# A linear-attention block whose feature blocks are cut at three heads, with the engines' order written anew

## The chip, the cores and the metric

The kernel runs on one core of one Trainium2 chip. The metric is device time in microseconds (us): the kernel before took 280.55 us, the median of three runs (280.23, 280.55 and 280.56). The profile is that of one execution. The engines are called as in the profile: PE multiplies matrices (PEld are its weight loads), DVE, ACT and POOL are the vector, scalar and general engines, SP issues DMAs; a q behind an engine's name marks what its sequencer does, such as issuing a DMA.

## The reference, cut to what matters

```python
def _A_ref(x, wqkv, w_phi, wo):          # x: 1 x 2048 x 640, H = 32 heads of Dh = 20
    q, k, v = ...                        # x @ wqkv, by heads
    pq = jnp.einsum("bhsd,hdf->bhsf", q, w_phi)
    pk = jnp.einsum("bhsd,hdf->bhsf", k, w_phi)
    phi_q = jnp.concatenate([_softmax(pq, axis=-1), _softmax(-pq, axis=-1)], axis=-1)
    phi_k = jnp.concatenate([_softmax(pk, axis=-1), _softmax(-pk, axis=-1)], axis=-1)
    kv = jnp.einsum("bhsf,bhsd->bhfd", phi_k, v)
    z  = jnp.einsum("bhsf->bhf", phi_k)
    num = jnp.einsum("bhqf,bhfd->bhqd", phi_q, kv)
    den = jnp.einsum("bhqf,bhf->bhq", phi_q, z)[..., None] + 1e-6
    o = num / den
    return (lambda x, *d: x.transpose(*d))(o, 0, 2, 1, 3).reshape(B, S, D) @ wo
...
h = x + _A_ref(_layernorm(x, axis=-1), A_wqkv, A_w_phi, A_wo)
h2 = h + _B_ref(_layernorm(h, axis=-1), B_w_gate, B_w_up, B_w_down)   # ((x@wg) * (x@wu)) @ wd, F = 1536
```

A head has 20 scores and, by softmax of both signs, 40 features. All heads together have 1280 features per token, and 32 x 21 columns of V with a column of ones, which gives the denominator.

## The kernel before, in words

The 2048 tokens are 16 tiles (t = 0 to 15) of 128. Everything that is matrix work goes through one helper, `mms` (line 570 is its matmul), so the profile names nearly all matmuls L570, and they are told apart by their tiles and columns. The weight of a matmul is always 128x128; what differs is the number of columns that move.

The work falls into units, and a unit's name is what the lists of the order use:

- `in`: first loads. On SP's list, in the order in which the code makes them: rows 0 of W_k (`load_wnat(1, (0, 1))`, 160 KB), rows 1 and 2 (320 KB), the transposed x tiles xT0 and xT1 (DMA transposes, `load_xT`), W_v (`load_wv`, 800 KB), xT2, xT3. On ACT's list: rows 3 and 4 of W_k (320 KB), then W_phi's rows (`Wrows`), then a first exp. On DVE and POOL: constants, masks and the block-diagonal `Phi`, which is made from `Wrows`. `lT4` to `lT15` are the further xT tiles, `lx0` to `lx3` the x rows by four tiles, `lwq`, `lwo`, `lg`, `lu`, `ld` weights, `t0` to `t4` DMA transposes of W_q.
- `wk`, ten entries on PE: for each of five row blocks of W_k a sum of its columns and a turn (transposes on PE, L659). Blocks 0 and 1 are copied out by DVE (L697) and ACT (L700, ACT's first `wk`). `lwq` writes W_q into the buffer `Wnat` that W_k lies in, and so comes after all five turns.
- `x0` to `x4`: W_k times `Phi`, evicted to `Wp`. `wv`, `c0` to `c4`: W_v is centred. `s0, s2, s4, s8, s12`: layer-norm sums of the batches of tiles from xT (`s0` is tiles 0 and 1, `s2` tiles 2 and 3). `y0` to `y4`: W_q times `Phi`.
- `k`t: scores of K (ten matmuls of 320 columns), a maximum (DVE), two exps (ACT) into `phik`; `K`t normalizes them (DVE sum and reciprocal, POOL product). `v`t: V, into `vaug`. `A`t: K^T V of two tiles, accumulated over all tiles in one PSUM buffer. `Aout`: its eviction with the mask `Gk` and the epsilon, to `KVsb` (L905, L908).
- `q`t and `Q`t: the same for the queries, into `eq`, which two DMA transposes bring to `phiqT`. `n`t: phi_q KV, division, and the turn to `oT`. `h`t: the product with W_o, the residual and sums for the second layer norm. `f`b.ft.j: gate and up product of four (or two) tiles, `d`t and `e`t: down product, residual, store.

The features of a tile are cut at every 128, without regard to heads, so a block touches up to four heads (SL = 4): its K^T V has 4 x 21 = 84 columns. `HQ[c]` is the first head of block c, and `Gk` zeroes what belongs to other heads. Ten blocks make a tile, in K^T V (`kv_mm`) as in phi_q KV (`num`).

The order is written out by hand for each engine in `ORDER`: an entry takes the next operation of that unit on that engine. `Prog.place` goes through the lists with a cost model (durations t, latencies) to choose buffers, and `Prog.finish` puts semaphore waits where an operation depends on one of another engine. Each engine works through its list in order, so an entry that waits holds what stands behind it. A DMA issue that waits holds the later issues of its engine too. A load's landing is, in the cost model,

```python
land = o.at or max(s + 2.3, fabric) + o.bytes
```

with `at` a landing time given in the code for the first loads (`load_wnat(1, (3, 5), "ACT", at=4.3)` and the others of `in`). DMAs go through rings of eight semaphores: an issue waits for the eighth one before it of its ring.

Of the kernel before, what the change touches and what calls it, by code (L numbers as in the profile page):

```python
# [34 lines left out]

# [342 lines left out]
def _build(ctx, nc, A_x, A_wqkv, A_w_phi, A_wo, B_w_gate, B_w_up, B_w_down, out):  # L378
# [437 lines left out]
    def softexp(v, t, i, dst, regs_, use=()):
        mx = lambda: PS[v.i][:, 1, MXC:MXC + 1]
        g.op("DVE", lambda e: e.tensor_reduce(out=mx(), in_=PS[v.i][:, :, 0:HALF], axis=AX.XY, op=ALU.max,  # L818
                                              apply_absolute_value=True, negate=True), rd=v.R, wr=[R_mx[i]], use=[v],
             t=0.735, lat=0.85)  # L820
        g.op("DVE", lambda e: e.tensor_tensor(out=nb[:, i:i + 1], in0=mx(), in1=rs[:, t:t + 1], op=ALU.mult),  # L821
             rd=[R_mx[i], R_rs[t]], wr=[R_nb[i]], use=[v], t=0.1, lat=0.24)
        for s in range(2):
            sc = rs if s == 0 else nrs
            g.op("ACT", lambda e, s=s, sc=sc: e.activation(  # L825
                out=signed(dst(), s), in_=PS[v.i][:, :, 0:HALF].rearrange("p b (h f) -> p b h f", f=DH), func=ACT.Exp,
                bias=nb[:, i:i + 1], scale=sc[:, t:t + 1]), rd=v.R + [R_nb[i], R_rs[t], R_nrs[t]], wr=[regs_[s]], use=[v] + list(use),
                t=0.775, lat=0.92)
# [68 lines left out]
    def kv_out():  # L897
        U("Aout")
        v = KVBUF
        for k in range(2):  # L900
            dst = KVsb[:, NC * KVW * k:NC * KVW * (k + 1)].rearrange("p (c h e) -> p c h e", c=NC, e=E21)

            def psv(k=k):
                return PS[v.i][:, k, 0:NC * KVW].rearrange("p (c h e) -> p c h e", c=NC, e=E21)
# [211 lines left out]
```

## Time and profile before

| | |
|---|---|
| runs | 280.23, 280.55, 280.56 us |
| span of the profiled execution | 278.3 us |
| PE busy | 274.1 us, 2239 matmuls |
| DVE / ACT / POOL busy | 165.3 / 134.5 / 106.2 us |
| warm-up matmuls at the start of PE | 0.83 to 5.04 us |
| first scores of K (128x320) | from 12.64 us |
| K^T V (128x84, 160 matmuls) | in groups from 64 to 74.4 us |
| phi_q KV (128x84, 160 matmuls) | 74.4 to 191.1 us |

A line of the timeline gives start and length in us, the engine, the line, the operation, what it writes and reads, and how many instructions are merged; a bracket tells how long the engine was idle before and what ended that. A line of groups ends in total busy time, mean length of one in ns, and idle time before. A line of DMA issues ends in the size of one and the median time from issue to landing. A matmul's length includes its passage through the array, so that the spacing of starts, not the length, is what a stream of them costs.

### The profile page before, as it was taken

To read this page: it belongs to the slowest core of one execution; us is meant where nothing else is said; L and a number is where in the kernel's file an instruction comes from. 1 tells how busy PE (TensorE), PEld (TensorE's weight loads), DVE (VectorE), ACT (ScalarE), POOL (GpSimd) and SP (SyncE) were. 2 spreads that over 40 slices of the span, in tenths; PEclk is the share of its full clock that TensorE was granted. 3 is DMA by queue.
4 is the path that set the end of the run, shared out by engine and by line. 5 is a ranking of instruction groups with operands and counts; after the bars stand their busy time and mean duration, and the time that the engine had idled before them with its cause. 6 is when DMAs were issued, how large, how long until landed. Compare 5 with 4: busy or idle time off the path is not lost.

```text
span 278.3 us, 5485 instructions
## 1 busy us (share of the span) xinstructions
PE 274.1 (99%) x2239; PEld 186.9 (67%) x2239; DVE 165.3 (59%) x314; ACT 134.5 (48%) x229; POOL 106.2 (38%) x150
## 2 busy tenths in 40 slices
PE   8999999999999999999999999999999999999995
PEld 8877777777878888877656555776464444447773
DVE  1999999999999876588545845313251222324011
ACT  3478999899666465421764413113244314340132
POOL 5438889899732240061320903142100000250252
PEclk9999999999999999999999999999999999999999
DMA  7988886008864617969643031544312000000112
GB/s 196 277 148 185 126 271 251 0 2 236 167 82 110 97 27 155 336 100 198 88 111 82 24 71 27 123 89 97 94 30 20 0 0 2 0 24 24 49 47 71
DMA packets 65193, 28.06 MB, mean 101 GB/s; under 512 B 55697, under 2 KB 63889, under 8 KB 65169
## 3 DMA queue, kind: packets, MB, share of 16 engines
q1 hardware_dynamic: 64240, 27.37, 43.8%
q10 hardware_dynamic: 928, 0.35, 0.5%
q8 instruction: 17, 0.28, 0.4%
q14 instruction: 8, 0.06, 0.1%
HBM read 11.82 MB, written 2.62 MB: 52 GB/s over the span
## 4 chain that ended last, share of the span: by engine, by line
PE 95%; DMA 2%; SPq 1%; DVE 1%; issue 0%
PE ps L570 95%; DMA Wp<-in_A_wqkv_dram 2%; SPq L471 1%; PE ps L482 0%; DVE outb L1022 0%; SPq L467 0%; DVE KVsb L905 0%; DVE KVsb L908 0%; DVE nb L821 0%
## 5 line engine op out<-in xcount | busy, mean ns | idle before, releaser
L570 PE MATMUL ps<-phik,Wgu 128*128 128x512 bf16 (+1 forms) x600 | 107.5, 336 | 0.0
L570 PEld LDWEIGHTS ps<-phik,Wgu 128*128 128x128 bf16 x600 | 58.2, 98 | 43.6 <-DVE phik L981 1.8
L570 PE MATMUL ps<-Wp,xT 128*128 128x320 bf16 x480 | 69.0, 299 | 0.0
L981 DVE TENSOR_TENSOR phik<-ps,gate 128x512 bf16<-128x512 f32 (+1 forms) x60 | 33.9, 577 | 55.3 <-PE ps L570 50.1
L570 PE MATMUL ps<-vaug,phik 128*128 128x320 bf16 (+3 forms) x544 | 60.0, 270 | 0.0
L979 ACT ACTIVATE gate<-ps 128x512 bf16<-128x512 f32 (+1 forms) x60 | 29.8, 510 | 59.7 <-PE ps L570 40.8
L570 PEld LDWEIGHTS ps<-Wp,xT 128*128 128x128 bf16 x480 | 45.9, 98 | 17.6 <-DVE phik L981 0.2
L570 PEld LDWEIGHTS ps<-vaug,phik 128*128 128x128 bf16 x544 | 43.7, 97 | 15.7
L839 POOL TENSOR_TENSOR phik<-phik,Rk 128x1280 bf16<-128x1280 bf16 x16 | 37.5, 2356 | 5.1 <-DVE Rk L838 4.8
L997 POOL TENSOR_TENSOR outb<-t,x_all 128x640 bf16<-128x640 f32 x12 | 16.8, 1397 | 56.9 <-ACT t L994 49.6
L994 ACT ACTIVATE t<-ps,mh,rs 128x640 f32<-128x640 f32 x12 | 10.6, 882 | 37.1 <-PE ps L570 37.1
L818 DVE TENSOR_REDUCE ps<-ps 128x1 f32<-128x640 f32 x32 | 26.3, 824 | 1.6 <-PE ps L570 1.2
L858 DVE TENSOR_REDUCE Sq<-eq 128x64 f32<-128x1280 bf16 x16 | 23.5, 1471 | 3.5 <-ACT eq L825 3.5
L825 ACT ACTIVATE eq<-ps,nb,rs 128x640 bf16<-128x640 f32 x16 | 14.2, 885 | 20.3 <-DVE nb L821 11.7
L836 DVE TENSOR_REDUCE Ssum<-phik 128x64 f32<-128x1280 bf16 x16 | 23.5, 1474 | 0.0
L964 POOL TENSOR_SCALAR vpe<-shc 128x1 f32<-128x1 f32 x16 | 3.0, 190 | 52.7 <-ACT junk L563 51.7
L869 POOL TENSOR_TENSOR eq<-eq,rq 128x640 bf16<-128x640 bf16 x16 | 20.2, 1270 | 0.5
L864 POOL TENSOR_TENSOR rq<-Sq,rq 128x32 f32<-128x32 f32 x16 | 4.0, 254 | 41.5 <-DVE rq L863 41.5
L563 ACT ACTIVATE junk<-x_all 128x640 bf16<-128x640 bf16 x20 | 14.6, 732 | 4.4 <-DVE x_all L958 4.4
L825 ACT ACTIVATE phik<-ps,nb,rs 128x640 bf16<-128x640 f32 x16 | 14.2, 889 | 2.4 <-DVE nb L821 2.4
L825 ACT ACTIVATE phik<-ps,nb,nrs 128x640 bf16<-128x640 f32 x16 | 14.3, 894 | 0.0
L825 ACT ACTIVATE eq<-ps,nb,nrs 128x640 bf16<-128x640 f32 x16 | 14.2, 885 | 0.0
(86 smaller groups left out, 235.8 us busy)
## 6 DMA issues: line engine op xcount, KB each, us to landing
x_all<-in_A_x_dram SPq DMA_DIRECT2D x4, 640.0 KB, 5.2
out_dram<-outb SPq DMA_DIRECT2D x15, 160.0 KB, 1.8
Wgu<-in_B_w_gate_dram SPq DMA_DIRECT2D x1, 1920.0 KB, 11.1
Wgu<-in_B_w_up_dram SPq DMA_DIRECT2D x1, 1920.0 KB, 9.1
vaug<-in_B_w_down_dram SPq DMA_DIRECT2D x1, 1920.0 KB, 8.3
Wp<-in_A_wqkv_dram SPq DMA_DIRECT2D x1, 800.0 KB, 4.9
phiqT<-in_A_wqkv_dram SPq DMA_DIRECT2D x1, 800.0 KB, 6.5
Wo<-in_A_wo_dram SPq DMA_DIRECT2D x1, 800.0 KB, 6.8
```

The lines of the kernel that those rows point to most:

```text
L563: g.op("ACT", lambda e: e.activation(out=junk[:, v.i, :], in_=in_, func=func, accum_out=acc), rd=rd, wr=wr, use=[v], t=0.73, lat=0.97)
L570: ins = e.matmul(o_, lhsT=l_, rhs=r_, start=s_, stop=p_, skip_group_check=True)
L818: g.op("DVE", lambda e: e.tensor_reduce(out=mx(), in_=PS[v.i][:, :, 0:HALF], axis=AX.XY, op=ALU.max, apply_absolute_value=True, negate=Tru ...
L825: g.op("ACT", lambda e, s=s, sc=sc: e.activation(out=signed(dst(), s), in_=PS[v.i][:, :, 0:HALF].rearrange("p b (h f) -> p b h f", f=DH), ...
L836: g.op("DVE", lambda e: e.tensor_reduce(out=Ssum[:, vs.i, :], in_=x, axis=AX.X, op=ALU.add), rd=R_phik[t], wr=vs.R, use=[vs], t=1.39, lat=1.5)
L839: g.op("POOL", lambda e: e.tensor_tensor(out=x, in0=x, in1=Rk[:, vr.i, :].unsqueeze(2).to_broadcast([P, 2 * H, DH]), op=ALU.mult), rd=vr.R ...
L858: g.op("DVE", lambda e: e.tensor_reduce(out=Sq[:, vs.i, :], in_=eq[:, b.i, :].rearrange("p (g f) -> p g f", f=DH), axis=AX.X, op=ALU.add), ...
L869: return e.tensor_tensor(out=x, in0=x, in1=rq[:, vr.i, :].unsqueeze(2).to_broadcast([P, H, DH]), op=ALU.mult)
L979: g.op("ACT", lambda e: e.activation(out=gate[:, vg.i, 0:P * n], in_=PS[v.i][:, 0, 0:P * n], func=ACT.Copy), rd=[v.R[0]], wr=vg.R, use=[v, ...
L981: g.op("DVE", lambda e: e.tensor_tensor(out=hhT[:, hb, ft, sl], in0=PS[v.i][:, 1, 0:P * n], in1=gate[:, vg.i, 0:P * n], op=ALU.mult), rd=[ ...
L994: g.op("ACT", lambda e: e.activation(out=t32[:, v3.i, :].rearrange("p (b n) -> p b n", b=2), in_=PS[v.i][:, :, 0:HALF], func=ACT.Identity, ...
L997: g.op("POOL", lambda e: e.tensor_tensor(out=outb[:, vo.i, :], in0=t32[:, v3.i, :], in1=x_all[:, t, :], op=ALU.add), rd=v3.R + [R_h[t]], w ...
```

## The change

Each block of 128 features now holds three heads and a pad of 8 features ahead of them: eleven blocks a tile (the last with two new heads; in K^T V it takes head 29 once more), 3 x 21 = 63 columns each. For K the pad is the 8 features ahead of the block in `BK`, for which 8 zero columns are put ahead of tile 0; for Q, `eq` is laid out with the pad, filled once with ones, and `Gk` has zero rows for it. In `num` the last block has two heads, 42 columns. The scores of the queries are split into 300 and 340 columns across two PSUM banks, their exps into two pieces for each sign, the transposes into five and six blocks. `KVsb` now lies where `Phi` was, and there is one `junk` buffer in place of two. The lists of the order are new for all five engines.

```diff
 DF = 2 * DH
-NQ = 2 * NC
-HQ = [P * c // DF for c in range(NQ)]
-SL = 4
-KVW = SL * E21
+HW = 3
+NQ = 11
+PADW = P - HW * DF
+KVW = HW * E21
+WB = ((0, 5), (5, NQ))
+HB = 5 * HW
...
     "PE":
-        "warm wk wk wk wk wk wk wk wk wk wk s0 s0 x1 x1 x3 wv wv x2 x0 x0 s2 s2 x4 k0 k0 k0 k0 k0 k1 k3 wm k2 v0 v2 s4 s4 "
+        "warm wk wk wk wk wk wk wk wk wk wk s0 x1 s0 x1 x3 wv wv x2 x0 x0 s2 x4 s2 k0 k0 k0 k0 k0 k1 k3 wm s4 s4 s4 s4 k2 k7 v2 "
...
-        "k12 v9 v12 v15 v14 k14 k15 A0 A2 A4 v8 q2 q3 A6 v10 A0 A2 A8 q5 A10 A4 A12 A6 A8 A10 A14 A12 A14 n1 n0 n0 n1 q7 "
+        "v15 k13 k15 v8 q2 v13 v10 q3 A0 A2 A4 A0 q5 A2 A6 A4 A8 A10 A6 A8 A12 A10 A14 A12 A14 n1 n0 n1 q7 n0 n1 q4 n0 h1 h0 n2 "
...
     "ACT":
-        "in in in wk wk wk x2 x0 x4 k0 k0 wm k1 k1 k3 k3 k2 k2 v0 wq3 v2 v3 wq1 v7 k7 k7 y2 k4 k4 v5 s12 v4 y0 s12 s12 k6 "
+        "wk in in wk wk in x2 x0 x4 s12 s12 k0 k0 wo2 wm k1 k1 k3 k3 k2 k2 wq1 v2 wq3 k7 k7 v3 v7 v0 k4 k4 y0 v5 y2 k6 s12 k6 "
...
     "SP":
-        "in in in in in in in lwq t4 lT7 lT4 t2 lT5 lT6 t3 t1 t0 lx3 lT10 lT15 lT9 lT11 lT8 lT13 lT14 lT12 lx0 lwo lg Q0 "
...
+        "lT7 in lT5 lx3 lT4 in lwo lT6 lwq lT8 lT15 t4 t0 t1 t2 t3 lT10 in lT11 in lT9 lT12 in in lx2 in lT14 lT13 lu Q0 lx1 lg "
...
-    BK = sb([P, 2 * NT * D], BF16, "phik")
+    BK = sb([P, PADW + 2 * NT * D], BF16, "phik")
...
-    affine([R_Gk], Gk[:, :, :], [[P - 3 * DF, NC], [-DF, SL]], 0, 1)
-    affine([R_Gk], Gk[:, :, :], [[3 * DF - P, NC], [DF, SL]], DF - 1, -1)
+    affine([R_Gk], Gk[:, :, :], [[0, 6], [-DF, HW]], -PADW, 1)
+    affine([R_Gk], Gk[:, :, :], [[0, 6], [DF, HW]], PADW + DF - 1, -1)
+    pool_op(lambda e: e.memset(eq[:, :, :].rearrange("p b (w n) -> p b w n", n=P)[:, :, :, 0:PADW], 1.0), 0.4, wr=[R_pad])
+    pool_op(lambda e: e.memset(eq[:, :, (NQ - 1) * P + PADW:(NQ - 1) * P + PADW + DF], 1.0), 0.2, app=[R_pad])
+    pool_op(lambda e: e.memset(BK[:, 0:PADW], 0.0), 0.1, wr=[R_pad0])
...
+            for k, (to, of, n) in enumerate(pieces):
+                g.op("ACT", lambda e, s=s, sc=sc, to=to, of=of: e.activation(
+                    out=to(s), in_=of(), func=ACT.Exp, bias=nb[:, i:i + 1], scale=sc[:, t:t + 1]),
...
+        for k, (w0, w1) in enumerate(WB):
+            transpose(lambda w0=w0, w1=w1: phiqT[:, bb, w0:w1, P * tt:P * (tt + 1)], lambda w0=w0, w1=w1: eq[:, b.i, P * w0:P * w1],
+                      b.R + [R_pad], [R_phiqT[bb][k][tt]], [b], t=0.254 * (w1 - w0), size=0.214 * (w1 - w0))
...
-                for c in range(NC * k, NC * (k + 1)):
-                    lo = HQ[c]
-                    col = KVW * (c - NC * k)
+                for w in range(w0, w1):
+                    h0 = min(HW * w, H - HW)
                     for t in range(t0, t1):
-                        o_ = (t * H + lo) * E21
-                        lst.append((PS[v.i][:, k, col:col + KVW], phik[:, t, P * c:P * (c + 1)], BV[:, o_:o_ + KVW], first, False))
+                        k0, o_ = 2 * D * t + HW * DF * w, (t * H + h0) * E21
+                        if w == NQ - 1:
+                            k0 -= DF
+                        lst.append((PS[v.i][:, k, KVW * (w - w0):KVW * (w - w0 + 1)], BK[:, k0:k0 + P], BV[:, o_:o_ + KVW], first, False))
...
-                for c in range(NC * b0, NC * b1):
-                    bk = c // NC
-                    col = E21 * (HQ[c] - HH2 * bk)
-                    lst.append((PS[v.i][:, bk, col:col + KVW], phiqT[:, bb, c, P * tt:P * (tt + 1)], KVsb[:, KVW * c:KVW * (c + 1)],
-                                c % NC == 0, False))
+                for bk in range(b0, b1):
+                    for w in range(*WB[bk]):
+                        k0 = KVW * w + (E21 if w == NQ - 1 else 0)
+                        o_ = base + KVW * w
+                        n = KVW * (w + 1) - k0
+                        lst.append((flat(v)[:, o_:o_ + n], phiqT[:, bb, w, P * tt:P * (tt + 1)], KVsb[:, k0:k0 + n], w == WB[bk][0], False))
```

Between these, the other lists (DVE, POOL, and the rest of the three above) are replaced as a whole; which operations they hold, apart from the added ones, is the same. The landing times `at` of the first loads are not touched.

More of the change, by code (lines that the diff above doesn't have):

```diff
@@ L425, in _build @@
     Rk = sb([P, 2, 2 * H], FP32, "Rk")
-    Sq = sb([P, 2, 2 * H], FP32, "Sq")
-    rq = sb([P, 2, H], FP32, "rq")
+    Sq = sb([P, 2, 2 * HW * NQ], FP32, "Sq")
+    rq = sb([P, 2, HW * NQ], FP32, "rq")
     rden = sb([P, 2, H], FP32, "rden")
-    phik = BK[:, :].rearrange("p (t n) -> p t n", t=NT)
+    Phi = PK[:, :].rearrange("p (a n) -> p a n", a=NC)
+    KVsb = PK[:, 0:NQ * KVW]
+    phik = BK[:, PADW:PADW + 2 * NT * D].rearrange("p (t n) -> p t n", t=NT)
     pq = phiqT[:, :, :, :].rearrange("p b c n -> p (b c n)")
@@ L824, in softexp @@
             sc = rs if s == 0 else nrs
[L825 to L828, printed above, removed]
+            for k, (to, of, n) in enumerate(pieces):
+                g.op("ACT", lambda e, s=s, sc=sc, to=to, of=of: e.activation(
+                    out=to(s), in_=of(), func=ACT.Exp, bias=nb[:, i:i + 1], scale=sc[:, t:t + 1]),
+                    rd=v.R + [R_nb[i], R_rs[t], R_nrs[t]], use=[v] + list(use),
+                    t=0.095 + 0.00106 * n, lat=0.235 + 0.00107 * n, **{"app" if k else "wr": [regs_[s]]})
     def keys(t, after=()):
         U("k%d" % t)
-        softexp(proj(t, 1, after), t, t, lambda: phik[:, t, :], R_phik[t])
+        v = proj(t, 1, after)
+        softexp(v, t, t, lambda: PS[v.i][:, :, 0:HALF],
+                [(lambda s: signed(phik[:, t, :], s), lambda: PS[v.i][:, :, 0:HALF].rearrange("p b (h f) -> p b h f", f=DH), D)],
+                R_phik[t])
         U("K%d" % t)
@@ L851, in queries, with score, feat @@
         U("q%d" % t)
-        v = proj(t, 0, after)
+        v = Buf(p_ps, 2)
+        cut = HB * DH
+        g.op("PE", lambda e: mms(e, [(flat(v)[:, 512 - cut:512] if bk == 0 else flat(v)[:, 512:512 + D - cut], xT[:, t, c, 0:P],
+                                      Wp[:, c, cut * bk:cut + (D - cut) * bk], c == 0, c == NC - 1)
+                                     for c in range(NC) for bk in range(2)]),
+             rd=[R_xT[t]] + R_Wp[0], wr=v.R, use=[v], t=1.3575, lat=1.5075, after=after)
         bb, tt = (t // 4) % 2, t % 4
         b = Buf(p_eq, 2)
-        softexp(v, t, NT + t, lambda: eq[:, b.i, :], b.R, [b])
+        def score(lo, hi):
+            return flat(v)[:, 512 - cut + lo:512 - cut + hi]
+        def feat():
+            return eq[:, b.i, :].rearrange("p (w n) -> p w n", n=P)[:, :, PADW:P]
+        softexp(v, t, NT + t, lambda: score(0, D),
+                [(lambda s: feat()[:, 0:NQ - 1, :].rearrange("p w (h s f) -> p s w h f", s=2, f=DH)[:, s],
+                  lambda: score(0, 2 * cut).rearrange("p (w h f) -> p w h f", h=HW, f=DH), 2 * cut),
+                 (lambda s: feat()[:, NQ - 1, DF:].rearrange("p (h s f) -> p s h f", s=2, f=DH)[:, s],
+                  lambda: score(2 * cut, D).rearrange("p (h f) -> p h f", f=DH), D - 2 * cut)], b.R, [b])
         vs, vr = Buf(p_Sq), Buf(p_rq)
         U("Q%d" % t)
-        g.op("DVE", lambda e: e.tensor_reduce(out=Sq[:, vs.i, :], in_=eq[:, b.i, :].rearrange("p (g f) -> p g f", f=DH),
-                                              axis=AX.X, op=ALU.add), rd=b.R, wr=vs.R, use=[b, vs], t=1.4, lat=1.5)
+        g.op("DVE", lambda e: e.tensor_reduce(out=Sq[:, vs.i, :].rearrange("p (w g) -> p w g", w=NQ),
+                                              in_=feat().rearrange("p w (g f) -> p w g f", f=DH),
+                                              axis=AX.X, op=ALU.add), rd=b.R + [R_pad], wr=vs.R, use=[b, vs], t=1.44, lat=1.54)
         def sums(k):
@@ L867, in f @@
         def f(e):
-            x = eq[:, b.i, :].rearrange("p (h s f) -> p s h f", s=2, f=DH)[:, 1, :, :]
-            return e.tensor_tensor(out=x, in0=x, in1=rq[:, vr.i, :].unsqueeze(2).to_broadcast([P, H, DH]), op=ALU.mult)
-        g.op("POOL", f, rd=vr.R + [b.R[1]], wr=[b.R[1]], use=[b, vr], t=1.25)
-        for k in range(2):
-            transpose(lambda k=k: phiqT[:, bb, NC * k:NC * (k + 1), P * tt:P * (tt + 1)], lambda k=k: eq[:, b.i, D * k:D * (k + 1)],
-                      b.R, [R_phiqT[bb][k][tt]], [b])
+            x = feat().rearrange("p w (h s f) -> p s w h f", s=2, f=DH)[:, 1]
+            return e.tensor_tensor(out=x, in0=x, in1=rq[:, vr.i, :].rearrange("p (w h) -> p w h", h=HW).unsqueeze(3).to_broadcast(
+                [P, NQ, HW, DH]), op=ALU.mult)
+        g.op("POOL", f, rd=vr.R + [b.R[1], R_pad], wr=[b.R[1]], use=[b, vr], t=1.29)
+        for k, (w0, w1) in enumerate(WB):
+            transpose(lambda w0=w0, w1=w1: phiqT[:, bb, w0:w1, P * tt:P * (tt + 1)], lambda w0=w0, w1=w1: eq[:, b.i, P * w0:P * w1],
+                      b.R + [R_pad], [R_phiqT[bb][k][tt]], [b], t=0.254 * (w1 - w0), size=0.214 * (w1 - w0))
     KVBUF = Buf(p_ps, 2)
@@ L899, in kv_out, with psv @@
         v = KVBUF
[L900 to L904, printed above, removed]
-            g.op("DVE", lambda e, psv=psv, dst=dst: e.tensor_tensor(
-                out=dst[:, :, :, 0:DH], in0=psv()[:, :, :, 0:DH], in1=Gk[:, :, :].unsqueeze(3).to_broadcast([P, NC, SL, DH]), op=ALU.mult),
-                rd=[v.R[k], R_Gk], app=[R_KV[k]], use=[v], t=0.5, lat=0.6)
-            g.op("DVE", lambda e, psv=psv, dst=dst: e.scalar_tensor_tensor(
-                out=dst[:, :, :, DH], in0=psv()[:, :, :, DH], scalar=0.5 * EPS_DEN, in1=Gk[:, :, :], op0=ALU.add, op1=ALU.mult),
+        for k, (w0, w1) in enumerate(WB):
+            n = HW * (w1 - w0)
+            dst = KVsb[:, KVW * w0:KVW * w1].rearrange("p (h e) -> p h e", e=E21)
+            gk = Gk[:, :, :].rearrange("p w h -> p (w h)")[:, 0:n]
+            def psv(k=k, n=n):
+                return PS[v.i][:, k, 0:E21 * n].rearrange("p (h e) -> p h e", e=E21)
+            g.op("DVE", lambda e, psv=psv, dst=dst, gk=gk, n=n: e.tensor_tensor(
+                out=dst[:, :, 0:DH], in0=psv()[:, :, 0:DH], in1=gk.unsqueeze(2).to_broadcast([P, n, DH]), op=ALU.mult),
+                rd=[v.R[k], R_Gk], app=[R_KV[k]], use=[v], t=0.07 + 0.0213 * n, lat=0.18 + 0.0213 * n)
+            g.op("DVE", lambda e, psv=psv, dst=dst, gk=gk: e.scalar_tensor_tensor(
+                out=dst[:, :, DH], in0=psv()[:, :, DH], scalar=0.5 * EPS_DEN, in1=gk, op0=ALU.add, op1=ALU.mult),
                 rd=[v.R[k], R_Gk], app=[R_KV[k]], use=[v], t=0.09, lat=0.25)
@@ L928, in f @@
                 return mms(e, lst)
[L929 to L930 removed]
+            n = sum(WB[bk][1] - WB[bk][0] for bk in range(b0, b1)) * 0.0288 + 0.015
+            g.op("PE", f, rd=R_KV[b0:b1] + [R_phiqT[bb][k][tt] for k in range(b0, b1)], wr=v.R[b0:b1], use=[v], t=n, lat=0.15 + n)
         for b0, b1 in halves:
[L932 to L935 removed]
@@ L937, in rd_ @@
[L937 to L944 removed]
+            h0, h1 = (0, HB)[b0], (0, HB, H)[b1]
@@ L1067, in _build @@
         kv_mm(t, t + 2)
+    g.alias(R_KV, R_Phi)
     kv_out()
```

52 lines of the change are left out of this document (25 added, 27 removed), and 77 rows, old and new, of the table ORDER.

## The prediction, on record before the run

> **What bounds the kernel now.** I read the page first, then the chain of waits in order of time, then busy time by stretches, and last the timelines of the engines in the first microseconds.
>
> ```profile
> span 278.3 us, 5485 instructions
> PE 274.1 (99%) x2239; PEld 186.9 (67%) x2239; DVE 165.3 (59%) x314; ACT 134.5 (48%) x229; POOL 106.2 (38%) x150
> ```
>
> The span is 278.3 us and the runs have a median of 280.55, so 2.25 us lie around the span; I add my terms to 280.55, as if the profiled execution were the median one. PE is busy all the time, but matmuls overlap their tails, so that alone does not say that PE's columns are the limit. The chain of waits does:
>
> ```profile
> 0.79 0.40 SPq L467
> ...
> 4.38 4.94 DMA Wp<-in_A_wqkv_dram
> 9.32 0.05 issue
> 9.37 27.97 PE ps L570 x283
> ...
> 74.38 0.58 DVE KVsb L905
> ...
> 84.13 190.70 PE ps L570 x1322
> ...
> 274.85 1.02 DVE outb L1022 x2
> ```
>
> (columns: start, length, what.) Up to 9.32 us the end is set by SP's issues and by the landing of W_v; from 9.37 to 274.85 by PE's own stream, with one hole, where the two Aout evictions stand at 74.4. Busy time in the stretches before and after that hole:
>
> ```profile
> core 0: us, PE busy (x) PEld busy (x) DVE busy (x) ACT busy (x) POOL busy (x), PEclk, DMA share, GB/s
> 9.37:74.36 64.99, 64.95 (x689) 49.89 (x689) 63.61 (x118) 55.27 (x87) 53.26 (x56) 1.00 0.69 163
> 75.17:274.85 199.68, 199.60 (x1416) 128.25 (x1417) 96.69 (x178) 75.95 (x137) 48.40 (x74) 1.00 0.35 75
> ```
>
> PE has no slack in either (64.95 of 64.99, 199.60 of 199.68). Two things follow: every PE microsecond saved is a microsecond, and **whatever delays the start of PE's stream can't be caught up later**.
>
> **The matmuls that change.** Timeline of PE:
>
> ```profile
> 66.90 1.52 PE L570 MATMUL ps<-Wp,xT 128*128 128x320 bf16 x10
> 68.26 1.30 PE L570 MATMUL ps<-vaug,phik 128*128 128x84 bf16 x30
> 69.40 1.52 PE L570 MATMUL ps<-Wp,xT 128*128 128x320 bf16 x10
> ...
> 81.58 0.55 PE L570 MATMUL ps<-KVsb,phiqT 128*128 128x84 bf16 x10
> 81.97 1.52 PE L570 MATMUL ps<-Wp,xT 128*128 128x320 bf16 x10
> 40.41 0.64 PE L570 MATMUL ps<-ones,xT 128*128 128x1 bf16 x20
> ```
>
> ```profile
> L570 PE MATMUL ps<-ones,xT 128*128 128x1 bf16 x20 | 0.6, 163 | 0.0
> ```
>
> From start to the next group's start: 320 columns 1.36/10 = 136 ns; 84 columns 1.14/30 = 38 ns in K^T V and 0.39/10 = 39 ns in phi_q KV. The slope between is 98/236 = 0.415 ns a column, so 63 columns are 38 - 21 x 0.415 = 29.3 ns. From below, 20 matmuls of one column, each with its own weights, take (0.64 - 0.16)/19 = 25 ns each, the 0.16 being the length of the last one; from above, no gain a piece, 38 ns. K^T V per tile: 10 x 38 = 380 -> 11 x 29.3 = 322. phi_q KV: the eleventh has 42 columns, taken as 25: 390 -> 318. Over 16 tiles: 16 x (58 + 72) = **-2.1 us**. Ends: at 25 ns each -3.6, at 38 ns each +1.0.
>
> The Trainium skill, "TensorE: Matmul & The Clock Gate", section "LDWEIGHTS (loading the stationary operand)", speaks against this edit: a weight load takes its 128 columns divided by 1.2 GHz, 107 ns, however few columns follow. By it eleven loads instead of ten would cost 32 x 107 ns = +3.4 us (an estimate from that page). The trace doesn't bear it out as a spacing: twenty loads with one column each are spaced 25 ns.
>
> **The other parts of the edit.** Aout: four evictions of fewer heads, and in the new order the first half is complete three PE groups ahead of the end (A12, A14 of the other half between), so the hole of 0.8 us at 74.4 shrinks: -0.3 (between 0 and -0.8). Queries: two activations become four (600 and 40 of 640 elements), so 32 short ones more; the row below gives about 0.2 us each, 6.4 us of ACT. The six-block transpose instead of five adds a fifth of 1.27 us to 16 SP issues, 4 us of SP. DVE's sum over 66 groups instead of 64 and POOL's product over 33 heads instead of 32 add 3%, and three memsets on POOL lie where it waits for W_phi. After 75 us ACT is busy 75.95 of 199.68 and SP waits for data; PE's stream covers all this. Ahead of Aout four tiles' queries would add 8 x 0.2 = 1.6 us to ACT, which has 64.99 - 55.27 = 9.7 idle: 0, and +1.6 without that cover.
>
> ```profile
> L797 ACT ACTIVATE Wo<-wsum 128x1 bf16<-128x1 f32 x5 | 1.0, 220 | 0.0
> ```
>
> **The new order at the head, the large term.** Here each DMA issue counts. SP and ACT issue in the order written. Before:
>
> ```profile
> 0.79 0.87 SPq L467 DMA_DIRECT2D phiqT<-in_A_wqkv_dram  x2
> 1.72 2.62 SPq L471 DMA_TRANSPOSE xT<-in_A_x_dram  x2
> 4.38 0.59 SPq L467 DMA_DIRECT2D Wp<-in_A_wqkv_dram  x1
> 5.01 2.55 SPq L471 DMA_TRANSPOSE xT<-in_A_x_dram  x2
> 7.60 0.58 SPq L467 DMA_DIRECT2D phiqT<-in_A_wqkv_dram  x1
> 22.81 12.10 SPq L471 DMA_TRANSPOSE xT<-in_A_x_dram  x8
> 0.78 0.45 ACTq L467 DMA_DIRECT2D phiqT<-in_A_wqkv_dram  x1
> 6.18 0.70 ACT L700 ACTIVATE phiqT<-ps 128x640 bf16<-128x640 bf16 x1 [2.90 <-PE ps L659]
> ```
>
> So a transpose holds SP for 1.31 us at the head and 1.51 in a long row; a plain load for 0.45 to 0.63. Landing, in us from the issue:
>
> ```profile
> x_all<-in_A_x_dram SPq DMA_DIRECT2D x4, 640.0 KB, 5.2
> Wp<-in_A_wqkv_dram SPq DMA_DIRECT2D x1, 800.0 KB, 4.9
> phiqT<-in_A_wqkv_dram ACTq DMA_DIRECT2D x1, 320.0 KB, 3.7
> phiqT<-in_A_wqkv_dram SPq DMA_DIRECT2D x1, 320.0 KB, 4.3
> xT<-in_A_x_dram SPq DMA_TRANSPOSE x16, 4.4
> phiqT<-in_A_wqkv_dram SPq DMA_DIRECT2D x1, 160.0 KB, 2.9
> ```
>
> And PE's head:
>
> ```profile
> 0.83 4.21 PE L570 MATMUL ps<-const-bfloat16-1.0 128*128 128x128 bf16 x38 [0.83 <-PEq L1101]
> 5.55 0.29 PE L570 MATMUL ps<-ones,phiqT 128*128 128x1 bf16 x5
> 6.58 0.27 PE L570 MATMUL ps<-ones,phiqT 128*128 128x1 bf16 x5
> 7.11 0.44 PE L659 MATMUL ps<-ident,phiqT 128*128 128x128 bf16 x5
> 12.64 3.57 PE L570 MATMUL ps<-Wp,xT 128*128 128x320 bf16 x25
> ```
>
> In the new lists SP begins lT7, W_k rows 0, lT5, lx3, lT4, W_k rows 1-2, lwo, lT6, lwq, lT8, lT15, t4, t0, t1, t2, t3, lT10, xT0, lT11, xT1, lT9, lT12, W_v, xT2, lx2, xT3; and ACT does wk's copy of row block 1 *ahead* of its load of W_k rows 3-4. Followed through:
>
> 1. W_k rows 1-2 are issued after three transposes (3.9), a load of 0.45 and one of 0.6 at 0.79 + 5.1 = 5.9, and land 4.3 later: 10.2.
> 2. PE turns block 1, ACT copies it: 6.18 - 5.55 = 0.63 and 0.70, so ACT issues rows 3-4 at 11.5; landed at 15.2. Before, that issue stood at 0.78.
> 3. PE turns blocks 3 and 4: 7.11 + 0.44 - 6.58 = 0.97, to 16.2. lwq overwrites W_k's buffer and so waits for this; **everything behind it on SP waits too**, xT0 to xT3 and W_v among it, for which PE waits. lwq is out at 16.8.
> 4. Eight transposes (lT8 to lT10) at 1.31 to 1.51, say 1.45: xT0 is issued at 28.4.
> 5. Five more (xT0, lT11, xT1, lT9, lT12), 7.25: W_v at 35.7, landed 40.6.
> 6. W_v's 0.63, xT2 1.45, lx2 0.6: xT3 is issued at 38.4, landed 42.8 by the median, 43.9 if it queues behind lx2's 5.2 us. PE's order has s2 on xT2 and xT3 ahead of k0, and from W_v to k0 it has 12.64 - 9.37 = 3.3 us of work, 43.9. k0 starts at 43.7, against 12.64: **+31.1 us**, and nothing behind it has slack.
>
> Ends: with 1.31 a transpose, 2.9 for rows 1-2, k0 is at 39.9 (+27.3); with 1.55, 5.2 for every landing and a queue behind lx2, at 46.5 (+33.9).
>
> After a wait the matmuls may be slow again: the first 38 of 128 columns take 4.05/38 = 107 ns, about twice what 0.415 ns a column gives (53). A second such start costs at most the same 2.0 us; 0 if the 3.3 us of work ahead of k0 bring the speed back. I take +1.0. The Trainium skill says it more strictly ("TensorE: Matmul & The Clock Gate", section on the HAM clock gate): after an idle window of about 3.4 us the clock is halved, until about 3.4 us of work have passed. By that, an estimate is +1.7 us here; the trace of before has no such wait after its start, so it can't tell.
>
> Sum: 280.55 - 2.1 - 0.3 + 31.1 + 1.0 = **310.3 us**. Own range, both ends of each term: 280.55 - 3.6 - 0.8 + 27.3 + 0 = 303.5 to 280.55 + 1.0 + 0 + 33.9 + 2.0 = 317.5.
>
> **The rivals.** *The wait at the head is made good* (the other side): the rest of PE's stream shrinks by as much as it starts late, because K and V tiles, all landed by then, run without waits. For it: DMA is at 0.69 up to 74 us. Against: PE's 64.95 of 64.99 are columns, not waits. Time if the start cost nothing: 280.55 - 2.4 = 278.2; it decides from where the delay is under 2.4 us, which six issues of 1.3 already pass. Chance 0.02.
>
> *lwq does not hold SP* (its wait falls early, as rows 3-4 come sooner): then lwq is out at 8.9 after lT6 instead of 16.8, all behind it 7.9 earlier: 302.4. For it: with SP blocked the DMA queues are empty and loads land fast. Against: rows 3-4 can't be issued ahead of ACT's copy. Chance 0.06, with anything between this and the first rival.
>
> *A second hole*: the late start is as computed, but the rewritten lists open holes in PE later, ahead of Aout above all, where DVE is busy 63.61 of 64.99 and can't make good a late tile. 5% of that stretch is +3.3 us, 10% +6.5: 314 to 317, beyond 318 with more. For it: that stretch has two engines at their limit. Against: the work on DVE is the same. Chance 0.12, half of it beyond 318.
>
> **How the numbers follow.** The forecast has 0.80. The range 303 to 318 leaves out the first two rivals (0.08), half of the third (0.06) and some 0.05 of the forecast's own tails. What a measurement can tell from no change is 0.2%, 0.56 us: slower 0.97, faster 0.02, same 0.01; all but the first rival are slower.
>
> **What would show it.** In the profile of the changed kernel: the chain in order of time has SP and DMA up to about 40 us, with lwq's wait in it; PE's first slices are nearly empty; the first 128x320 group stands at 43.7 instead of 12.64; K^T V groups have starts 29 ns apart; from there to the end there are 262 - 2 us of dense PE. Wrong it is if PE's 320-column stream starts before 38 us, if PE has holes over 3 us behind it, or if 63 columns are spaced 38 ns.

## The result, and the profile after

The changed kernel takes 314.32 us (median of five runs, 313.56 to 315.17), the kernel before in the same place 280.49: a ratio of 1.1216, 95% interval [1.1199, 1.1232], so 33.8 us slower. The spans of the two profiled executions differ by 312.8 - 278.3 = 34.5 us, and they are compared below. The page of the changed kernel:

```profile
span 312.8 us, 5594 instructions
...
PE 278.8 (89%) x2271; PEld 188.2 (60%) x2271; DVE 169.8 (54%) x314; ACT 142.2 (45%) x261; POOL 108.7 (35%) x153
...
PE   5210389899999999999999999999999999999996
...
PEclk9555559999999999999999999999999999999999
```

The third line shows PE's busy tenths in 40 slices of 7.8 us: the second to the fifth are nearly empty, and from the seventh on they are as full as before. The fourth line is the granted clock: half speed from the second slice to the sixth, which the page of before never shows. Next its chain of waits in order of time (start, length, what):

```profile
0.79 1.30 SPq L473
...
5.91 5.10 DMA phiqT<-in_A_wqkv_dram
11.95 3.23 DMA phiqT<-in_A_wqkv_dram
17.18 1.22 SPq L473
...
31.65 1.27 SPq L473
32.97 1.95 SPq L473
34.96 5.11 DMA Wp<-in_A_wqkv_dram
40.12 7.32 PE ps L575 x54
```

W_k's rows 1-2 land at 11.01, rows 3-4 (ACT's) at 15.2, then SP issues thirteen transposes one after the other until W_v can go out at 34.96; it lands at 40.07. Before, W_v was issued at 4.38 and landed at 9.32. What PE did meanwhile (timeline; the bracket is the idle time ahead and what ended it):

```profile
11.05 0.29 PE L575 MATMUL ps<-ones,phiqT 128*128 128x1 bf16 x5 [5.35 <-DMA phiqT<-in_A_wqkv_dram]
...
15.22 0.30 PE L575 MATMUL ps<-ones,phiqT 128*128 128x1 bf16 x5 [2.65 <-DMA phiqT<-in_A_wqkv_dram]
...
31.15 0.72 PE L575 MATMUL ps<-xT 128*128 128x129 bf16 x5 [14.42 <-DMA xT<-in_A_x_dram]
...
34.93 0.72 PE L575 MATMUL ps<-xT 128*128 128x129 bf16 x5 [2.46 <-DMA xT<-in_A_x_dram]
...
40.12 2.85 PE L575 MATMUL ps<-Wp,ones 128*128 128x320 bf16 x10 [3.27 <-DMA Wp<-in_A_wqkv_dram]
...
45.91 4.24 PE L575 MATMUL ps<-Wp,xT 128*128 128x320 bf16 x30
...
102.38 1.40 PE L575 MATMUL ps<-vaug,phik 128*128 128x63 bf16 x42
103.61 1.53 PE L575 MATMUL ps<-Wp,xT 128*128 128x300 bf16 x10
...
116.95 0.51 PE L575 MATMUL ps<-Phi,phiqT 128*128 128x63 bf16 x11
117.30 1.53 PE L575 MATMUL ps<-Wp,xT 128*128 128x300 bf16 x10
...
120.95 4.31 PE L575 MATMUL ps<-phik,Wgu 128*128 128x256 bf16 x38
```

(The profile names KVsb by the buffer it now shares, Phi.) The first scores of K, k0, start at 45.91 instead of 12.64: +33.3 us. Busy time from there, cut at the first gate and up product; first the changed kernel, then the kernel before:

```profile
core 0: us, PE busy (x) PEld busy (x) DVE busy (x) ACT busy (x) POOL busy (x), PEclk, DMA share, GB/s
45.91:120.95 75.04, 73.00 (x789) 54.05 (x786) 72.64 (x141) 65.07 (x110) 56.31 (x58) 1.00 0.35 91
120.95:309.40 188.45, 188.45 (x1320) 119.55 (x1318) 88.26 (x155) 72.50 (x144) 45.38 (x67) 1.00 0.35 69
```

```profile
12.64:85.87 73.23, 72.86 (x767) 55.61 (x766) 71.73 (x142) 61.60 (x96) 54.82 (x56) 1.00 0.64 144
85.87:274.80 188.93, 188.93 (x1307) 120.11 (x1305) 86.15 (x154) 68.28 (x126) 45.16 (x69) 1.00 0.34 74
```

The first stretch is 75.04 instead of 73.23, +1.8, with 2.0 us in which PE isn't busy instead of 0.4. From 120.95 to the span's end it is 191.8 instead of 192.4, -0.6. Together 33.3 + 1.8 - 0.6 = 34.5, the difference of the spans. So the head makes the loss; but the rest, where 2.4 us should have been gained, loses 1.2 too, and that asked for experiments of its own.

### The profile page after: what moved, and what is told of

It is laid out like the page before. It is cut to its first block, busy times and chain, and to the rows that moved or that the text cites. A ratio compares the mean times of both kernels' runs of the same rounds, so it can differ in the third digit from the quotient of the medians.

```text
span 312.8 us, 5594 instructions
## 1 busy us (share of the span) xinstructions
PE 278.8 (89%) x2271; PEld 188.2 (60%) x2271; DVE 169.8 (54%) x314; ACT 142.2 (45%) x261; POOL 108.7 (35%) x153
## 4 chain that ended last, share of the span: by engine, by line
PE 72%; SPq 8%; ACT 6%; DVE 6%; DMA 6%; issue 2%; POOL 1%; ACTq 0%
PE ps L575 71%; SPq L473 7%; ACT phik L834 3%; DMA phiqT<-in_A_wqkv_dram 3%; ACT eq L834 3%; DMA Wp<-in_A_wqkv_dram 2%; DVE ps L826 2%; DMA phiqT<-eq 1%; DVE Ssum L848 1%; DVE phiqT L742 1%; ACT vaug L857 1%; PE ps L664 1%; DVE Sq L886 0%; SPq L469 0%; POOL eq L898 0%
## 5 line engine op out<-in xcount | busy, mean ns | idle before, releaser
L575 PE MATMUL ps<-Wp,xT 128*128 128x320 bf16 (+1 forms) x480 | 69.3, 299 | 0.8 <-ACT eq L834 0.4
L1015 DVE TENSOR_TENSOR phik<-ps,gate 128x512 bf16<-128x512 f32 (+1 forms) x60 | 34.5, 580 | 47.8 <-PE ps L575 37.5
L575 PEld LDWEIGHTS ps<-Wp,xT 128*128 128x128 bf16 x480 | 45.4, 97 | 20.1 <-ACT phik L834 1.5
L575 PEld LDWEIGHTS ps<-vaug,phik 128*128 128x128 bf16 x560 | 42.5, 98 | 15.8 <-DVE phik L1015 0.2
L1031 POOL TENSOR_TENSOR outb<-t,x_all 128x640 bf16<-128x640 f32 x12 | 16.8, 1398 | 78.6 <-ACT t L1028 78.5
L886 DVE TENSOR_REDUCE Sq<-eq 128x66 f32<-128x1320 bf16 x16 | 24.2, 1514 | 4.7 <-ACT eq L834 4.6
L1028 ACT ACTIVATE t<-ps,mh,rs 128x640 f32<-128x640 f32 x12 | 10.5, 885 | 33.5 <-PE ps L575 33.5
L834 ACT ACTIVATE eq<-ps,nb,rs 128x600 bf16<-128x600 f32 (+1 forms) x32 | 18.5, 619 | 13.1 <-DVE nb L829 13.1
L893 POOL TENSOR_TENSOR rq<-Sq,rq 128x33 f32<-128x33 f32 x16 | 4.1, 258 | 50.8 <-DVE rq L892 49.3
L898 POOL TENSOR_TENSOR eq<-eq,rq 128x660 bf16<-128x660 bf16 x16 | 20.9, 1309 | 0.8
L575 PE MATMUL ps<-xT 128*128 128x129 bf16 x60 | 5.4, 243 | 16.9 <-DMA xT<-in_A_x_dram 16.9
L834 ACT ACTIVATE eq<-ps,nb,nrs 128x600 bf16<-128x600 f32 (+1 forms) x32 | 18.2, 631 | 0.0
L771 ACT ACTIVATE Wp<-ps 128x640 bf16<-128x640 f32 x6 | 4.2, 700 | 26.5 <-PE ps L575 26.5
L575 PE MATMUL ps<-Phi,phiqT 128*128 128x63 bf16 (+3 forms) x236 | 14.3, 209 | 1.3 <-DVE phiqT L742 0.9
```

The source lines that it names most:

```text
L575: ins = e.matmul(o_, lhsT=l_, rhs=r_, start=s_, stop=p_, skip_group_check=True)
L834: g.op("ACT", lambda e, s=s, sc=sc, to=to, of=of: e.activation(out=to(s), in_=of(), func=ACT.Exp, bias=nb[:, i:i + 1], scale=sc[:, t:t + 1 ...
L886: g.op("DVE", lambda e: e.tensor_reduce(out=Sq[:, vs.i, :].rearrange("p (w g) -> p w g", w=NQ), in_=feat().rearrange("p w (g f) -> p w g f ...
L898: return e.tensor_tensor(out=x, in0=x, in1=rq[:, vr.i, :].rearrange("p (w h) -> p w h", h=HW).unsqueeze(3).to_broadcast([P, NQ, HW, DH]), ...
L1015: g.op("DVE", lambda e: e.tensor_tensor(out=hhT[:, hb, ft, sl], in0=PS[v.i][:, 1, 0:P * n], in1=gate[:, vg.i, 0:P * n], op=ALU.mult), rd=[ ...
L1028: g.op("ACT", lambda e: e.activation(out=t32[:, v3.i, :].rearrange("p (b n) -> p b n", b=2), in_=PS[v.i][:, :, 0:HALF], func=ACT.Identity, ...
```

## The experiments

**The head put back, whole and in halves.** `head_back` moves tokens of two lists of the changed kernel and nothing else; `sp_back` has SP's move alone, `act_back` ACT's alone.

```diff
     "ACT":
-        "wk in in wk wk in x2 x0 x4 s12 s12 k0 k0 wo2 wm ...
+        "in in in wk wk wk x2 x0 x4 s12 s12 k0 k0 wo2 wm ...
     "SP":
-        "lT7 in lT5 lx3 lT4 in lwo lT6 lwq lT8 ...
+        "in in in in in in in lT7 lT5 lx3 lT4 lwo lT6 lwq lT8 ...
```

> The changed kernel with only its first loads moved back: SP issues the seven loads of in first, ACT the two of in ahead of wk; all else of the new lists stays. If the head wait is the whole loss: k0 starts at about 12.6 us again and 314.3 - 33.3 = 281.0 us, with the new lists' later holes (2.8 us more than before) still in; 278.2 if those holes come from the late start. If the three-head blocks or the rest of the lists cost by themselves: over 290.

> The changed kernel with only ACT's loads ahead of its first wk. lwq then waits for W_k rows 1-2 (11.0 us) alone: issued at about 12.4 instead of 16.8, k0 at 41.5, 309.9 us. Rival (lwq's wait does not hold SP): no change, 314.3.

> The changed kernel with only SP's seven loads first; ACT's loads stay behind its wk copy. W_k rows 3-4 go out at about 6.9 us, land at 10.5, turns done at 11.7, W_v long there: k0 at 15.5 to 17, 314.3 - 30 = 284 us. Rival (ACT's late load is the larger part): over 295.

Measured: `head_back` 289.73 us (ratio to before 1.0331 [1.0307, 1.0354]), `act_back` 312.98, `sp_back` 288.76 (the two halves are one execution each). Timeline of PE of `head_back`, and its busy time by stretches (columns as above: length, PE, PEld, DVE, ACT, POOL, granted clock, DMA share, GB/s):

```profile
12.66 4.25 PE L575 MATMUL ps<-Wp,xT 128*128 128x320 bf16 x30
22.49 0.82 PE L575 MATMUL ps<-ones,phiqT 128*128 128x1 bf16 x25 [5.59 <-DMA phiqT<-in_A_wqkv_dram]
```

```profile
16.90:22.50 5.60, 0.01 (x2) 0.01 (x1) 2.36 (x3) 2.48 (x6) 0.83 (x2) 0.98 1.15 254
22.50:25.00 2.50, 2.50 (x43) 2.50 (x44) 0.00 (x0) 1.65 (x3) 0.00 (x0) 0.50 1.01 189
...
27.00:29.00 2.00, 2.00 (x9) 1.11 (x8) 0.79 (x2) 0.48 (x1) 0.00 (x0) 0.50 0.77 163
29.00:31.00 2.00, 2.00 (x16) 1.44 (x15) 2.00 (x8) 1.44 (x2) 1.21 (x4) 0.98 0.71 119
```

k0 is back at 12.66, and 24.6 of the 33.8 us with it. I had forecast 281: moving the seven loads ahead left lwq behind lT7, lT5, lx3, lT4, lwo and lT6, so that W_q landed late and wm, which sums it, held PE for 5.6 us, and then the clock was at half speed until 29 us. It is one more wait of the same kind, a load that stands too far back in SP's list. The halves show what holds what. With ACT's loads alone ahead, lwq goes out at 14.55 instead of 16.77 us and all shifts by a little (k0 44.3, -1.3 us in time); I had forecast 12.4 and 309.9, but all four turns now stand behind the landing of rows 1-2 (11.6), at 0.65 us each. With SP's alone ahead, W_v is there early and k0 stands at 20.1, behind the turn of rows 3-4; forecast were 15.5 to 17 and 284, but rows 3-4 landed at 12.0 and not at 10.5, and the clock was at half speed there until 17.5. SP's order has most of the loss; where it is right, ACT's still moves k0 by 20.1 - 12.7 = 7.4 us, which the two times don't show, as lwq's hole in `head_back` takes it back.

**lwq out of the way.** `lwq_late` takes the changed kernel and moves one token of SP's list behind xT3.

```diff
     "SP":
-        "lT7 in lT5 lx3 lT4 in lwo lT6 lwq lT8 lT15 t4 t0 t1 t2 t3 lT10 in lT11 in lT9 lT12 in in lx2 in lT14 ...
+        "lT7 in lT5 lx3 lT4 in lwo lT6 lT8 lT15 t4 t0 t1 t2 t3 lT10 in lT11 in lT9 lT12 in in lx2 in lwq lT14 ...
```

> The changed kernel with lwq moved behind xT3 on SP's list, so that its wait holds neither xT0 nor W_v. Theory: all of that is issued 8.1 us earlier: k0 at 38, 306 us. Rival (SP is not held by lwq's wait, or the DMAs are the limit there): 314.

Measured: 308.53 us; W_v issued at 28.60 instead of 34.96, k0 at 39.9. This is one execution. So lwq's wait does hold all behind it, and its share is some 5.8 us of the 33.8, less than the 8.1 forecast: the thirteen transposes ahead of W_v take 19.4 us of SP here (9.2 to 28.6) instead of 17.8, as two of them take 2.4 us where most take 1.3, and W_v lands 6.0 us after its issue instead of 5.1. That more data under way slows them is my reading, not tested. These transposes are the larger part of the loss.

**The head alone.** `old_blocks_new_head` is the kernel before, blocks of 128 features and its lists, but with the head of SP's list (up to lT13) and of ACT's as in the changed kernel.

> The kernel before, blocks of 128 features and all, with only the head of SP's and ACT's lists as in the changed kernel. If the head alone makes the loss: k0 at 45 to 46 us, 280.5 + 33 = 313.5 us. If the blocks share in it: under 305.

Measured, in one execution: 313.42 us, k0 at 45.24, as forecast. Its stretch from k0 to the first gate and up product:

```profile
45.24:118.49 73.25, 72.88 (x767) 55.63 (x766) 71.75 (x142) 61.78 (x96) 54.84 (x56) 1.00 0.31 85
```

73.25 us, where the kernel before has 73.23. The head by itself makes the whole step of 33 us, and a late start leaves this stretch as it was: nothing is made good, and nothing is lost in it either. (From the first gate and up product to the end it is 193.2 us instead of 192.4; 0.6 of that is one wait of PE for DVE.) The 1.8 us that the changed kernel loses in this stretch are therefore its own.

**The clock held up.** `keep_pe_running` puts matmuls of constants into PE's three long waits of the changed kernel.

```diff
+    def keep(v, n):
+        one = nc.const_aps.tensor(1.0, (P, P), BF16)
+        g.op("PE", lambda e: mms(e, [(PS[v.i][:, 1, 384:512], one, one, True, True) for _ in range(n)]),
+             wr=[v.R[1]], use=[v], t=0.056 * n, lat=0.056 * n + 0.15)
```

> The changed kernel with matmuls of constants put into PE's three waits (215 of 128 columns ahead of the first s0, 40 ahead of the second, 60 ahead of wv); they write a part of PSUM that nothing reads. Theory: the granted clock stays at 1 through the waits, W_v to k0 takes 3.3 us instead of 5.8: k0 at 43.4 to 44.6 (not ahead of xT3's landing at 44.5), 312.5 to 313 us. Rival (the 5.8 us are late data, not a slow clock): k0 at 45.9 and 314.3.

Measured: 314.66 us (ratio to before 1.1226 [1.1208, 1.1245]), no gain. Timeline of PE:

```profile
41.41 1.53 PE L575 MATMUL ps<-Wp,ones 128*128 128x320 bf16 x10 [0.87 <-DMA Wp<-in_A_wqkv_dram]
...
44.88 0.46 PE L575 MATMUL ps<-xT 128*128 128x129 bf16 x5 [0.34 <-DMA xT<-in_A_x_dram]
45.18 2.88 PE L575 MATMUL ps<-Wp,xT 128*128 128x320 bf16 x20
48.62 1.53 PE L575 MATMUL ps<-Wp,xT 128*128 128x320 bf16 x10 [0.57 <-DVE Wp L801]
49.99 0.77 PE L575 MATMUL ps<-ones,phiqT 128*128 128x1 bf16 x25
```

The time is that of the rival, not the 312.5 to 313 forecast, though the clock is up as forecast: W_v's sums take 1.37 us instead of 2.64 (from start to the next group), W_v to k0 3.8 instead of 5.8. But W_v landed 1.3 us later in this execution, k0 then waited for xT3 and later for DVE, and wm starts at 49.99, against 49.98 in the changed kernel. What the slow clock costs when data and DVE don't bind stays open here; it was not the cause of the 33 us.

**The blocks with other lists.** `old_order` has the three-head blocks with all lists of before (each q entry of ACT twice, three more entries of in on POOL). `blocks_new_lists` has lists made for the blocks, with the loads of in kept first; `head_fitted` has the changed kernel's lists with a head in the sequence of before.

> Three-head blocks, with the lists of before (each q entry of ACT doubled, three more in entries on POOL). Theory: the blocks alone save 1.5 us (63-column matmuls spaced 30 ns): 279.0 us, range 278.3 to 279.6, first 128x320 group at 12.6 us. Rival: the extra activations and the six-block transposes open holes of 2 to 3 us ahead of Aout: 281 to 282.

> Three-head blocks, the new lists, but their head put in the sequence of before: SP with the seven loads of in, then lwq, t4, lT7, lT4, lT5, lT6 and on; ACT with its loads first, s12 and wo2 put behind later keys since their data comes later. lwq lands near 14 us, so the hole of 5.6 us that head_back had ahead of wm goes, and with it the slow clock behind it. k0 at 12.7 us. Theory (head alone is the loss, 1.5 us gained by the blocks, the new lists' holes of some 2.8 us ahead of Aout stay): 281.5 us. If those holes come from the late start: 278.8.

> Three-head blocks with lists of their own for all engines, rearranged from those of before under one condition: the seven loads of in stay first on SP, the three entries of in first on ACT. If the loss lay in the head and the rest in lists that don't fit the blocks' longer work on ACT: 1.5 us less on PE and few new holes, 279.0 to 280.0 us, ratio 0.995 to 0.999. If the blocks themselves cost (extra exps, six-block transposes): 282 us or more, as with the lists of before.

Measured: `old_order` 283.51 us (1.0101 [1.0074, 1.0128]), `head_fitted` 285.69 (1.0195 [1.0172, 1.0218]), `blocks_new_lists` 283.19 (1.0106 [1.009, 1.0122]). All three miss their forecasts of 279.0, 281.5 and 279 to 280. `head_fitted` and `blocks_new_lists` start k0 in time (12.97 and 12.91); in the profiled execution of `old_order`, its slowest at 286.88 us, W_v landed 2 us late and k0 stands at 16.25. PE's waits in `head_fitted` (columns: who waited for whom, us in total, times, longest):

```profile
PE ps L575 <- ACT phik L834: 2.0, 3, 0.8
PE ps L575 <- DVE phiqT L742: 1.2, 1, 1.2
PE ps L575 <- DMA xT<-in_A_x_dram: 1.2, 1, 1.2
```

In `head_fitted` the stretch from k0 to the first gate and up product is 79.4 us. One of these waits, for xT, is for data that this head brings later than the lists behind it count on; the one for DVE is taken up below, and whether ACT's come of that too is not tested. And the blocks lose 3 us even where lists were made for them, although PE's columns are fewer.

**What the blocks lose.** The groups of ACT in the changed kernel:

```profile
L834 ACT ACTIVATE eq<-ps,nb,nrs 128x600 bf16<-128x600 f32 x16 | 13.7, 861 | 0.0
L834 ACT ACTIVATE eq<-ps,nb,rs 128x600 bf16<-128x600 f32 x16 | 13.6, 852 | 13.1 <-DVE nb L829 13.1
L834 ACT ACTIVATE eq<-ps,nb,nrs 128x40 bf16<-128x40 f32 x16 | 6.3, 401 | 0.0
L834 ACT ACTIVATE eq<-ps,nb,rs 128x40 bf16<-128x40 f32 x16 | 6.1, 386 | 0.0
```

One of the two groups of before (the other has 885 ns too):

```profile
L825 ACT ACTIVATE eq<-ps,nb,rs 128x640 bf16<-128x640 f32 x16 | 14.2, 885 | 20.3 <-DVE nb L821 11.7
```

An exp of 40 elements takes 0.39 us, and 600 elements hardly less than the 640 of before: cutting costs (861 + 852 + 401 + 386) - 2 x 885 = 730 ns a tile. `split_exps` makes that cut in the kernel before, blocks and lists unchanged:

```diff
-    def softexp(v, t, i, dst, regs_, use=()):
+    def softexp(v, t, i, dst, regs_, use=(), cuts=((0, HH2),)):
...
-        softexp(v, t, NT + t, lambda: eq[:, b.i, :], b.R, [b])
+        softexp(v, t, NT + t, lambda: eq[:, b.i, :], b.R, [b], ((0, HH2 - 1), (HH2 - 1, HH2)))
```

> The kernel before, blocks of 128 features and all, with each query exp cut into 600 and 40 elements as the three-head blocks need, its q entries on ACT doubled, all else of the lists as before. If the extra 8 us of ACT are what opened the holes of old_order (283.5): 282 to 284 us. If not (six-block transposes, or the new blocks' sums): 280.3 to 280.8.

Measured: 282.38 us, 1.0075 [1.0062, 1.0088]: 2.15 us for that cut alone. The other way round, two kernels keep the blocks and make the exps whole again, by writing the 20 scores of head 29 twice:

```diff
+        parts = ((512 - cut, 0, cut), (512, cut, cut), (512 + cut, D - HW * DH, HW * DH))
...
+                [(lambda s: feat().rearrange("p w (h s f) -> p s w h f", s=2, f=DH)[:, s],
+                  lambda: score(0, D + DH).rearrange("p (w h f) -> p w h f", h=HW, f=DH), D + DH)], b.R, [b])
```

> Three-head blocks with the lists of before as in old_order (283.5), but the query exps whole again: the projection writes the 20 scores of head 29 a second time, between head 29 and head 30 (300 + 300 + 60 columns instead of 300 + 340), so that one exp of 660 elements for each sign fills all eleven blocks. PE pays 16 x 5 extra matmuls and 20 columns each, 1.1 us in all; ACT is spared 11 us of short instructions. If the cut exps are what the blocks lose: 281.0 to 281.8. If not: 283.5 to 284.6.

> The same whole exps with the lists of blocks_new_lists (283.2), which were made for cut ones. If the cut exps are what the blocks lose: 280.3 to 281.5, so level with the kernel before at best, as PE's 1.5 us of gain and 1.1 us of price nearly cancel. If not: 283 to 284.3.

Measured: 281.13 us (1.0039 [1.0026, 1.0051]) and 281.72 (1.0057 [1.0045, 1.0069]). With the lists of before, whole exps bring 283.51 to 281.13, -2.4 us (-2.2 when each is set against the kernel before measured beside it, 280.28 and 280.13), though PE has more columns. With the new lists they bring 283.19 to 281.72, -1.5 us, just short of the 280.3 to 281.5 forecast. The stretch from k0 to the first gate and up product in that kernel and in `split_exps`, in this order:

```profile
12.71:86.17 73.46, 72.62 (x832) 55.69 (x831) 71.92 (x142) 62.11 (x96) 55.02 (x56) 1.00 0.65 145
```

```profile
12.79:87.42 74.63, 73.65 (x769) 55.45 (x766) 71.79 (x142) 64.92 (x110) 54.92 (x57) 1.00 0.65 148
```

ACT has 61.6 us of work in the kernel before, 62.1 with whole exps, 64.9 with cut ones; DVE has the same 71.8 to 71.9 in both. With cut exps the stretch is 1.2 us longer. So ACT, at 84% of that stretch and not the bound by its share, still sets when DVE and PE get on. No kernel here beats the one before.

**A copy on DVE.** PE's longest wait in the changed kernel's stretch, 0.9 of its 2.0 us, is not for ACT. It is for a copy of W_q (L742) on DVE; lines of DVE, POOL and PE:

```profile
54.53 0.38 DVE L742 TENSOR_SCALAR phiqT<-phiqT,nmeanq 128x640 bf16<-128x640 bf16 x1
60.38 2.02 DVE L742 TENSOR_SCALAR phiqT<-phiqT,nmeanq 128x640 bf16<-128x640 bf16 x1
59.86 4.75 POOL L851 TENSOR_TENSOR phik<-phik,Rk 128x1280 bf16<-128x1280 bf16 x2 [2.18 <-DVE Rk L850]
62.45 0.49 PE L575 MATMUL ps<-Phi,phiqT 128*128 128x140 bf16 x6 [0.89 <-DVE phiqT L742]
```

The same copy takes 0.38 us at 54.53, where POOL has only a short operation on four columns, and 2.02 where it starts inside POOL's product (two are merged in that line), until the first of them ends. In the four profiles with the lists of before (`before`, `old_order`, `split_exps`, `one_exp_old_lists`) it takes 0.3 to 0.4 us each time, and no listed wait of PE is for it; in `blocks_new_lists` and `one_exp_new_lists` one takes about 2.5 us, again begun inside the product, and PE waits 0.6 for this line. That the product is the cause is argued from this agreement, as no run moves the copy alone; but it is a loss of the new order, not of the blocks.

## Why the prediction came out as it did

- *PE's start can't be caught up*: right, and shown by `old_blocks_new_head` (73.25 against 73.23 us behind a start 32.6 us later).
- *The head, step by step*: rows 1-2 landed at 11.0 (forecast 10.2), rows 3-4 at 15.2 (15.2), lwq issued at 16.8 (16.2), xT0 at 27.7 (28.4), W_v at 35.0 (35.7) and landed at 40.1 (40.6). The chain of SP's and ACT's issues was followed rightly, though rows 3-4 came on time by luck: rows 1-2 were 0.8 us late, and ACT's load landed in 3.2 us instead of 3.7. `lwq_late` confirms that lwq's wait holds the queue, with a share of 5.8 us. The ends were worked loosely: 5.2 us for every landing gives k0 at about 48 rather than 46.5, and 39.9 comes out only with 2.9 us for rows 3-4 too. The 45.9 measured lies inside either way.
- *From W_v to k0*: the term that was mis-sized. I took 3.3 us of work, and put the slow clock at +1.0 behind k0; it was 5.8, as PE ran the whole of it at half speed, and the clock was up at k0. k0 came at 45.9, not 43.7. How much of it runs slowly is in part chance: the same work took 4.6 us in `old_blocks_new_head` and 5.3 in `lwq_late`, for which see the last section. The Trainium skill's rule on the clock gate that the prediction cites is borne out in that the wait halved the clock; its estimate of +1.7 us stands against 2.5 (5.8 - 3.3).
- *The matmuls*: 42 of 63 columns in K^T V are spaced 1.23/42 = 29.3 ns, as forecast. In phi_q KV eleven take 0.35 us, 32 ns each, where 28.9 were forecast, so 40 ns a tile are saved and not 72: 16 x (58 + 40) = 1.6 us instead of 2.1. The Trainium skill's weight-load rule ("TensorE: Matmul & The Clock Gate", section "LDWEIGHTS (loading the stationary operand)") gives 107 ns as the duration of a load; read as a spacing, as the prediction's estimate did, it is contradicted, since each of these matmuls has its own load. As a duration the page of the changed kernel has 97 to 98 ns in its largest groups of loads.
- *The Aout hole*: the 0.3 us were not gained. PE loses about 0.4 us there before (75.17 - 74.41 - 0.39) and 0.5 now (109.88 - 109.09 - 0.32).
- *ACT's extra exps hidden by PE's stream, cost 0*: this step failed. I priced a short activation by a row of one element (0.2 us); 40 elements take 0.39. And I called ACT's idle time in the stretch its slack; `split_exps` puts the price at 2.15 us in time, and the whole exps give 2.4 back. The +1.6 that the prediction named for the case without cover was left out of its range. The rival of a second hole was thus partly true beside the forecast: 1.8 us behind k0, and the 1.0 that K^T V saves there on top, 2.8 us of later loss. In the changed kernel itself PE's idle time shows 1.7 of it (2.0 against 0.4); of the 2.0, 0.9 is for DVE's copy, some 0.7 for ACT and 0.3 for Aout's eviction. What ACT alone costs in its lists was not measured.
- *The sum*: 310.3 forecast, 314.3 measured: k0 +2.2 instead of the +1.0 that stood for the clock, the matmuls' gain 0.5 smaller, Aout's 0.3 not gained, 2.8 us of later loss not counted: 315.1, and the medians differ by 0.7 us less than the profiled spans do.

Why the new lists put the loads so late is read from the code, not tested: `place` takes a landing time `at` as given, whatever the issue time, and the loads pushed back are the ones that have it.

## What to carry to other kernels

On an engine that issues DMAs in order, a transfer with a wait, or a row of slow issues, delays every transfer behind it; follow the first bytes that the bounding engine needs through each queue, and don't let a cost model pin landing times that depend on the order. An engine's idle share is not free time where others wait for its results: here ACT was at 84% of a stretch, and 0.73 us more a tile cost 2.15 us. Price a split instruction by an instruction of about its size, and test it alone. A saving on the bounding engine, here 1.6 us of PE's columns, can be less than what the edit asks of the engines that feed it.
